# Loading the first group's x of a spectral filter and spatial-shift MLP kernel through two issuing engines

## The chip, the cores and the metric

The kernel runs on one core of a Trainium2 chip. The core has a matrix engine (PE, with its weight loads shown as PEld), a vector engine (DVE), an activation engine (ACT), a general engine (POOL) and a sync engine (SP) that issues the loads and stores; 16 DMA engines move the data. The metric is the device time of one execution in microseconds (us). Before the change it is 407.98, the median of three runs from 407.47 to 408.54.

## What is computed

The input x has 2048 rows of 448 channels. It is normalised over the channels, and the normalised rows go through two branches, whose results are added to x:

```python
x = A_x
xn = _layernorm(x, axis=-1)
return x + _A_ref(xn, A_w_r, A_w_i) + _B_ref(xn, B_w1, B_w2, B_w3, B_w4)
```

The first branch is a spectral filter: a two-dimensional real Fourier transform, a product with complex weights, and the inverse transform. The second is an MLP whose first steps are what the opening of the kernel works on; the part left out shifts each quarter of the channels of h by +1, -1, +2 or -2 rows, as g0 to g3:

```python
def _B_ref(x, w1, w2, w3, w4):
    h = _gelu(_layernorm(x, axis=-1) @ w1)
    ...
    hs = jnp.concatenate([g0, g1, g2, g3], axis=-1) @ w2
    x1 = x + hs
    h2 = _gelu(_layernorm(x1, axis=-1) @ w3) @ w4
    return x1 + h2
```

## The kernel before

**Tiling.** The 2048 rows are viewed as 128 partitions of 16 consecutive rows each; "block b" is row b of each partition, a tile of 128 x 448. Four groups of four blocks are formed (line 22): group 0 is blocks 14, 15, 0 and 1, and groups 1 to 3 follow with blocks 2 to 13. Each group has its own tile `xt[g]` of 128 x 4 x 448 in fp32. For group 0 the blocks lie in two places of x, so `load_x(0)` (lines 195 to 200) issues two loads of two blocks each; the other groups take one load each.

**The opening.** In the order of the source: a one-column tile `warm` is cleared by DVE and run through the gelu on ACT (lines 183 to 185), which makes ACT load its table at the start; DVE clears `wsrc`, the source of PE's warm-up products (line 188), and `ones`; POOL helps to build `ident`. Then SP issues the loads: x of group 0 (two), three pieces of w1 (line 206), its last 64 rows (207), x of group 1, the last 64 rows again into the other 64 partitions (209), w2 (210), x of group 2, and w3 in pieces with x of group 3 between them (221 to 223). PE runs 18 warm-up products of 128 x 512 (lines 900 to 906).

**The chain to the first product.** ACT squares the four pieces of w1 and sums them (lines 951 to 953); PE adds up the sums (`norm_of`, line 965), and DVE makes a power-of-two scale from the result (`factors`, lines 263 to 274). Meanwhile `norm1(0, ...)` (lines 341 to 408) takes each block's mean and variance on DVE (lines 326 and 327), a first guess of the reciprocal root (305) and the negative mean times it (362), and normalises the four blocks in place, three on DVE and one on POOL (370). PE transposes them (428), ACT and DVE split the transposed blocks into two fp16 parts (438, 439), the scaled w1 is split in the same way (281 and 283), and PE starts the products with w1 (479). These go on into w2, w3 and w4, with the Fourier transforms between them, to the end of the kernel.

**The order.** A planner sets the order on each engine. It simulates the program's times (`schedule_with_timeline_sim=True`, line 1220) and takes instructions by their place in the source as they become ready; `with behind(...)` blocks force an instruction behind another one on its engine. The planner also assigns semaphores: in the trace, eight of them serve the loads in turn.

Of the kernel before, what the change touches and what calls it, by code (L numbers as in the profile page):

```python
# [12 lines left out]
F32 = mybir.dt.float32  # L13
F16 = mybir.dt.float16
I32 = mybir.dt.int32
AF = mybir.ActivationFunctionType
# [5 lines left out]
GRP = [[14, 15, 0, 1], [2, 3, 4, 5], [6, 7, 8, 9], [10, 11, 12, 13]]  # L22
# [100 lines left out]
def body(tc, nc, x, wf, w1, w2, w3, w4, c_g, c_n, c_small, out):  # L123
    V, A, P, T, SY = nc.vector, nc.scalar, nc.gpsimd, nc.tensor, nc.sync
# [13 lines left out]
    def pool(name, bufs=1, side="left", space=None):  # L138
        kw = dict(name=name, bufs=bufs, reuse_waits="tile")
        if space is not None:  # L140
            kw["space"] = space
        else:
            kw["side"] = side
        cm = tc.tile_pool(**kw)
        opened[name] = cm
        return cm.__enter__()
# [9 lines left out]
    pc = pool("pc")  # L156
# [6 lines left out]
    xt = [px.tile([128, 4, D], F32, name=f"xt{i}") for i in range(4)]  # L163
# [5 lines left out]
    xv = x.rearrange("(a b) d -> a b d", b=NB)  # L169
    ov = out.rearrange("(a b) d -> a b d", b=NB)  # L170

    def stage(name, n, side, dtype=F32):
        t = pw.tile([128, 1808], F32, tag=f"stage{side}", bufs=1, name=name)
        return (t if dtype is F32 else t.bitcast(dtype))[:, :n]
# [5 lines left out]
        used[0] += 1  # L180
        return xr[:, 452 * (used[0] % 2):452 * (used[0] % 2) + 452]

    warm = pc.tile([128, 1], F32, name="warm")
    V.memset(warm, 0.0)
    A.activation(out=warm, in_=warm, func=AF.Gelu_apprx_tanh)
    x2mem = pw.tile([128, 9 * F], F16, name="x2mem")
    wsrc = x2mem[:, 8 * F:8 * F + 512]
    V.memset(wsrc, 0.0)
# [6 lines left out]
    def load_x(g):  # L195
        if g:
            SY.dma_start(xt[g], xv[:, GRP[g][0]:GRP[g][0] + 4])
        else:
            for i in (0, 2):
                SY.dma_start(xt[g][:, i:i + 2], xv[:, GRP[g][i]:GRP[g][i] + 2])  # L200

    load_x(0)
    w1s = stage("w1s", F, 0).rearrange("p (t n) -> p t n", t=4)
    w2s = stage("w2s", F, 1).rearrange("p (t n) -> p t n", t=4)
    for t in range(3):
        SY.dma_start(w1s[:, t], w1[128 * t:128 * t + 128])
    SY.dma_start(w1s[0:64, 3], w1[384:448])
    load_x(1)
    SY.dma_start(w1s[64:128, 3], w1[384:448])
    SY.dma_start(w2s[:112], w2)  # L210
    load_x(2)
    w3raw = pa.tile([128, 4, F], F32, tag="R", bufs=1, name="w3raw")

# [823 lines left out]
    for k in (1, 3):  # L1037
        with behind(0, 3):
            A.activation(out=w2p[:, 0, k], in_=w2s[:112, k], func=AF.Copy)
        with behind("np", 2):  # L1040
            i = P.tensor_tensor(out=w2p[:, 1, k], in0=w2s[:112, k], in1=w2p[:, 0, k], op=ALU.subtract)
# [182 lines left out]
```

## Time and profile before

| | |
|---|---|
| median of 3 runs | 407.98 us |
| lowest and highest | 407.47 and 408.54 us |
| profiled execution, its own time | 407.72 us |
| its span (first to last instruction) | 405.9 us |
| PE busy | 400.4 us (99%) |
| DVE, ACT, POOL busy | 304.2, 267.5, 170.1 us |
| granted TensorE clock | 1.0 |
| moved by DMA | 49.46 MB |

The profile records one execution. The span leaves out 1.8 us of that execution's own time, which lie around it. "Busy" counts the time in which an engine runs instructions that compute; issuing a load is not counted. The chain of waits is followed back from the last instruction: at each step to what released it, or to the instruction before it on its engine. In the rows of the timeline the columns are start, length, engine, line of the source, operation, written tile <- read tiles, count, and in brackets the idle time of the engine before the row with what ended it. Matmuls are pipelined, and a record of one is longer than its distance from the next.

### The profile page before, as it was taken

The page shows a single profiled execution, that of the slowest core. Times are in us where ns is not written, and L with a number is a line of the kernel's source. Part 1 is how long each engine was busy: PE and PEld are TensorE (multiplying, and loading weights), DVE is VectorE, ACT ScalarE, POOL GpSimd, SP SyncE. Part 2 cuts the span into 40 slices and gives each one's busy share as a digit, 9 for nine tenths or more (in the row PEclk, how much of TensorE's full clock was granted, in tenths as well). Part 3 has the DMA queues.
Part 4 walks back from the last instruction along what each step waited for, and adds up shares of the span by engine and source line. Part 5 has one row for each costly group of instructions (what it writes and reads, how often), then busy time and mean ns, then how long its engine had stood idle before and what let it go on. Part 6 is the DMA issues. An engine that isn't in the chain of part 4 may idle for free.

```text
span 405.9 us, 8826 instructions
## 1 busy us (share of the span) xinstructions
PE 400.4 (99%) x3383; PEld 296.7 (73%) x3383; DVE 304.2 (75%) x657; ACT 267.5 (66%) x464; POOL 170.1 (42%) x269
## 2 busy tenths in 40 slices
PE   8999999999999999999999999999999999999996
PEld 4555556666677877776878878877788888888885
DVE  5989999899645658884677777773588879889645
ACT  4699985874738766862687888776856566444332
POOL 2889911011397746599143344331232164221000
PEclk9999999999999999999999999999999999999999
DMA  8999999906910383427064566631000112233201
GB/s 282 364 267 186 172 178 246 274 2 131 232 48 1 97 277 129 115 39 173 15 157 120 144 158 158 155 94 57 2 1 2 31 61 76 94 108 94 89 2 45
DMA packets 57209, 49.46 MB, mean 122 GB/s; under 512 B 41312, under 2 KB 52192, under 8 KB 57168
## 3 DMA queue, kind: packets, MB, share of 16 engines
q1 hardware_dynamic: 57168, 48.91, 46.1%
q8 instruction: 26, 0.43, 0.4%
q14 instruction: 15, 0.12, 0.1%
HBM read 35.06 MB, written 3.67 MB: 95 GB/s over the span
## 4 chain that ended last, share of the span: by engine, by line
PE 86%; DVE 8%; DMA 3%; ACT 1%; issue 1%; SPq 0%; DVEq 0%
PE pw L449 28%; PE acc L826 22%; PE pw L524 9%; PE pw L479 8%; PE pu L722 3%; PE ps L619 3%; PE pp L676 2%; PE px L693 2%; PE cr L841 2%; PE acc L841 2%; DVE xr L574 1%; DMA out<-xr 1%; PE pe L742 1%; PE py L764 1%; DVE hf L792 1%
## 5 line engine op out<-in xcount | busy, mean ns | idle before, releaser
L449 PE MATMUL pw<-x2mem,w3p 128*128 128x256 f16 x1232 | 149.1, 272 | 0.0
L449 PEld LDWEIGHTS <-w3p 128*128 128x128 f16 x1232 | 118.7, 98 | 19.3
L826 PE MATMUL acc<-w4p,hf 128*128 128x448 f16 x508 | 107.4, 352 | 0.0
L826 PEld LDWEIGHTS <-hf 128*128 128x128 f16 x532 | 51.4, 98 | 35.6
L792 DVE SCALAR_TENSOR_TENSOR hf<-pw,h,hf 128x512 f16<-128x512 f32 x56 | 41.8, 747 | 36.2 <-ACT hf L791 35.8
L788 ACT ACTIVATE pw<-pw,pe 128x512 f32<-128x512 f32 x56 | 36.7, 655 | 44.0 <-PE pw L449 43.8
L791 ACT ACTIVATE hf<-pw,h 128x512 f16<-128x512 f32 x56 | 38.2, 683 | 1.2
L524 PE MATMUL pw<-w2p,h 112*128 112x448 f16 x192 | 38.9, 352 | 0.0
L749 POOL TENSOR_TENSOR e<-e 128x226 f32<-128x226 f32 x16 | 10.7, 669 | 64.3 <-ACT e L746 56.9
L479 PE MATMUL pw<-w1p,w4x 128*128 128x448 f16 x176 | 34.8, 352 | 0.5 <-DVE pe L270 0.5
L524 PEld LDWEIGHTS <-h 112*128 112x128 f16 x192 | 18.8, 98 | 15.6
L703 POOL TENSOR_TENSOR xr<-te 128x450 f32<-128x450 f32 x16 | 15.7, 980 | 34.1 <-DVE te L701 34.1
L479 PEld LDWEIGHTS <-w4x 128*128 128x128 f16 x176 | 17.1, 98 | 16.4 <-ACT w4x L438 0.7
L711 POOL TENSOR_TENSOR zb<-xr,zb 128x450 f16<-128x450 f32 x16 | 16.1, 1009 | 17.1 <-ACT zb L710 17.1
L756 ACT ACTIVATE vh<-e 128x448 f16<-128x448 f32 x16 | 9.2, 576 | 15.7 <-DVE e L754 15.6
L699 DVE SCALAR_TENSOR_TENSOR te<-px,sc,wc 128x450 f32<-128x450 f32 x16 | 11.0, 685 | 10.3 <-ACT te L698 6.7
L698 ACT ACTIVATE te<-px 64x450 f32<-64x450 f32 x32 | 17.2, 539 | 1.7 <-PE px L693 1.2
L734 ACT ACTIVATE U<-y 113x512 f16<-113x512 f16 x32 | 18.0, 620 | 0.1
L746 ACT ACTIVATE e<-pe 128x452 f32<-128x452 f32 x16 | 8.7, 544 | 13.0 <-PE pe L742 10.2
L726 DVE SCALAR_TENSOR_TENSOR y<-pu,y 113x512 f16<-113x512 f32 x16 | 10.9, 687 | 6.9 <-ACT y L725 6.8
L757 DVE TENSOR_TENSOR vh<-e,vh 128x448 f16<-128x448 f32 x16 | 10.0, 622 | 7.1 <-ACT vh L756 7.1
L683 ACT ACTIVATE pf<-pp 64x450 f16<-64x450 f32 x16 | 8.7, 541 | 9.7 <-PE pp L676 7.8
(205 smaller groups left out, 784.3 us busy)
## 6 DMA issues: line engine op xcount, KB each, us to landing
wc<-wf SPq DMA_DIRECT2D x32, 225.0 KB, 3.8
wl<-wf SPq DMA_DIRECT2D x8, 450.0 KB, 4.1
xt<-x SPq DMA_DIRECT2D x3, 896.0 KB, 10.8
w3raw<-w SPq DMA_DIRECT2D x3, 896.0 KB, 13.9
xf<-x SPq DMA_DIRECT2D x6, 448.0 KB, 3.8
xr<-x SPq DMA_DIRECT2D x12, 224.0 KB, 2.5
out<-xr SPq DMA_DIRECT2D x12, 224.0 KB, 2.0
gn<-c_g SPq DMA_DIRECT2D x16, 128.0 KB, 3.3
```

Of the source, the lines that this page charges most:

```text
L449: m = T.matmul(ps_out, wp[:, wi + t, cols], xT[:, xi + t, tok], start=t == 0 and wi + xi == 0, stop=t == 3 and wi == 4)
L479: m = T.matmul(pm[:, :D], xTs[g][:, xi + t, 128 * i:128 * i + 128], w1p[:, wi + t], start=t == 0 and p == 0, stop=t == 3 and p == 2)
L524: m = T.matmul(w2b[b][:, :D], hT[g][:112, 4 * hi + k, o:o + 128], w2p[:, wi, k], start=k == 2 and hi + wi == 0, stop=k == 3 and hi == 1)
L698: i = A.activation(out=e[64 * h:64 * h + 64], in_=px_[64 - 64 * h:128 - 64 * h, :2 * DF], func=AF.Copy)
L703: P.tensor_tensor(out=z, in0=t[:, 0], in1=t[:, 1], op=ALU.add)
L711: P.tensor_tensor(out=zv[1], in0=z, in1=zv[0], op=ALU.subtract)
L734: A.activation(out=U[b][:113, p].rearrange("p q (c k) -> p q c k", c=NC), in_=Y1[:113, p, :, :, b], func=AF.Copy)
L788: A.activation(out=pm, in_=pm, func=AF.Gelu_apprx_tanh, scale=r3)
L791: i = A.activation(out=h[:, 0], in_=pv_, func=AF.Copy, scale=h3)
L792: j = V.scalar_tensor_tensor(out=h[:, 1], in0=pv_, scalar=h3, in1=h[:, 0], op0=ALU.mult, op1=ALU.subtract)
L826: m = T.matmul(to, h[:, hi, 2 * f + i], w4p[0][:, wi, 2 * fp + f, r], start=fp == s and f == 0 and hi + wi == 0, stop=fp == e and f == 1 a ...
L841: m = T.matmul(to, h[:, hi, slot] if slot < 4 else g[:, hi, slot - 4], w4f[fp][k][wi], start=k in (0, 6) and fp == 0 and hi == 0, stop=hi ...
```

## The change

The second of the two loads of group 0 is issued by ACT (`A`) in place of SP (`SY`). The clearing of `warm` and its activation, which brings ACT's table load with it, move from ahead of the memsets to behind `load_x(0)`, so that ACT's issue stands ahead of them in the source. Nothing else is changed; the loads move the same bytes to the same places.

```diff
-    warm = pc.tile([128, 1], F32, name="warm")
-    V.memset(warm, 0.0)
-    A.activation(out=warm, in_=warm, func=AF.Gelu_apprx_tanh)
     x2mem = pw.tile([128, 9 * F], F16, name="x2mem")
     wsrc = x2mem[:, 8 * F:8 * F + 512]
     V.memset(wsrc, 0.0)
...
         if g:
             SY.dma_start(xt[g], xv[:, GRP[g][0]:GRP[g][0] + 4])
         else:
-            for i in (0, 2):
-                SY.dma_start(xt[g][:, i:i + 2], xv[:, GRP[g][i]:GRP[g][i] + 2])
+            for i, q in ((0, SY), (2, A)):
+                q.dma_start(xt[g][:, i:i + 2], xv[:, GRP[g][i]:GRP[g][i] + 2])

     load_x(0)
+    warm = pc.tile([128, 1], F32, name="warm")
+    V.memset(warm, 0.0)
+    A.activation(out=warm, in_=warm, func=AF.Gelu_apprx_tanh)
```

## The prediction

> **What bounds the kernel now.** I read the page first, for the engine that fills the span and for what lies outside it.
>
> ```profile
> span 405.9 us, 8826 instructions
> PE 400.4 (99%) x3383; PEld 296.7 (73%) x3383; DVE 304.2 (75%) x657; ACT 267.5 (66%) x464; POOL 170.1 (42%) x269
> ```
>
> PE is busy for 99% of the span, so time can be won or lost in three places only: before PE gets going, in holes between its matmuls, and after its last one. A split of the span into stretches (length, then busy time and count of each engine, granted clock, DMA share, GB/s) shows where the holes are.
>
> ```profile
> 2.00:3.00 1.00, 1.00 (x4) 0.40 (x3) 0.00 (x0) 0.21 (x2) 0.59 (x2) 1.00 0.64 179
> 3.00:4.00 1.00, 1.00 (x4) 0.36 (x3) 0.00 (x0) 0.00 (x0) 0.00 (x0) 1.00 0.93 362
> 6.00:13.00 7.00, 6.21 (x43) 4.36 (x42) 6.76 (x23) 5.05 (x13) 3.42 (x5) 1.00 1.05 327
> 13.00:20.00 7.00, 7.00 (x41) 3.94 (x40) 6.67 (x22) 3.93 (x6) 6.40 (x17) 1.00 1.00 397
> 20.00:30.00 10.00, 10.00 (x61) 5.67 (x59) 8.60 (x24) 9.23 (x18) 8.17 (x17) 1.00 1.10 271
> 40.00:405.90 365.90, 362.43 (x3180) 275.76 (x3178) 270.80 (x552) 237.85 (x413) 140.69 (x185) 1.00 0.41 105
> 402.70:405.90 3.20, 0.00 (x0) 0.00 (x0) 0.45 (x1) 0.00 (x0) 0.00 (x0) 1.00 0.41 143
> ```
>
> Between 13 and 30 us PE has no hole. From 40 us on it lacks 365.90 - 362.43 = 3.47 us, of which 3.20 is the stretch after its last matmul. About 0.3 us is left in all that time: whatever moves PE's first real matmul moves the end by the same amount. So the chain of waits over the first 11 us decides (start, length, what).
>
> ```profile
> 0.73 3.93 DMA xt<-x
> 4.66 0.02 issue
> 4.68 1.15 DVE sta L326 x2
> 5.84 0.22 DVE mva L327 x2
> 6.05 1.04 DVE sta L326 x2
> ...
> 7.95 1.87 DVE xt L370 x4
> ...
> 10.38 0.45 DVE w1p L281
> 10.84 0.07 DVE pe L270
> 10.91 0.07 issue
> 10.98 0.92 PE pw L479 x4
> ```
>
> The first link is the landing of the first half of group 0 (blocks 14 and 15) at 4.66. From there DVE works through 6.30 us without a break: statistics, normalisation, scale of w1, and PE's first product with w1 at 10.98. The second half (blocks 0 and 1) isn't a link: DVE goes from the first half's averages at 5.84 to the second half's statistics at 6.05 with no wait named. Asked for singly, the two issues (size, us from issue to landing) read
>
> ```profile
> xt<-x SPq DMA_DIRECT2D x1, 448.0 KB, 3.9
> xt<-x SPq DMA_DIRECT2D x1, 448.0 KB, 4.6
> ```
>
> and the first instructions in order of time (start, length)
>
> ```profile
> 0.73 1.28 ACT L185 ACT_TABLE_LOAD   x1 [0.73 <-PEq L1217]
> 0.80 0.06 DVE L184 MEMSET warm<- 128x1 f32 x1 [0.80 <-PEq L1217]
> 0.89 0.27 DVE L188 MEMSET x2mem<- 128x256 uint32 x1
> 1.19 0.42 SPq L200 DMA_DIRECT2D xt<-x  x1
> 1.66 0.42 SPq L206 DMA_DIRECT2D w1s<-w  x1
> 2.02 0.20 ACT L185 ACTIVATE warm<-warm 128x1 f32<-128x1 f32 x1
> 5.76 0.35 SPq L197 DMA_DIRECT2D xt<-x  x1
> 6.42 0.58 ACT L246 ACTIVATE xr<-w1s 128x448 f16<-128x448 f32 x1 [4.20 <-DMA w1s<-w]
> ```
>
> The second half, issued at 1.19, lands 4.6 later, near 5.74: 1.08 us after the first. 448 KB in 1.08 us is about 425 GB/s, close to what the stretches after 3 us show. The two halves come one behind the other at the pace of the DMA engines, and only the front one holds up DVE.
>
> **The change, part by part.**
>
> *One issue leaves SP.* The second half's row at 1.19 disappears there, and everything behind it comes 1.66 - 1.19 = 0.47 us sooner: the w1 pieces, x of group 1, w2, x of group 2, w3. This gains nothing: from 3 us on the DMA share is 0.93 to 1.10, so an earlier place in a full queue is no earlier landing. The squares of w1 on ACT wait for those pieces, and their norm meets DVE's chain here:
>
> ```profile
> 9.68 0.28 PE L967 MATMUL pm<-m,ones 128*128 128x1 f32 x2
> 10.01 0.15 DVE L265 TENSOR_SCALAR pe<-pm 128x1 int32<-128x1 int32 x1
> ```
>
> The norm's last product ends at 9.96 and DVE reads it at 10.01, so the two paths are level: an earlier w1 alone can't pull PE forward, nor does a w1 that comes no later hold up a DVE that starts later.
>
> *One issue enters ACT.* ACT issues for about 0.42 us (the row at 1.19), then loads its table for 1.28, then runs the one-column activation for 0.20: it is free at about 0.73 + 0.42 + 1.28 + 0.20 = 2.63 instead of 2.22. What hides this is its idle time of 4.20 us up to 6.42; without that cover it would cost 0.42. Behind the issue on ACT stands nothing but these two and the squares.
>
> *The memset of the one-column tile moves behind the others on DVE.* The 512-column source of PE's warm-up is cleared up to 0.09 us sooner (0.89 - 0.80), and PE's warm-up begins and ends as much sooner. It is worth nothing, since PE waits for the norm afterwards.
>
> *Loads that wait for earlier landings.* SP's tenth load (group 2's x) starts at 5.76, right after the second load landed at 5.74. If the ninth hangs on the first half in that way and that lands at 5.6, it goes out some 0.8 later than now. At that time nearly 1.5 MB (w1 and group 1's x) is still queued, over 3 us at 400 GB/s: no cost as long as that queue is there.
>
> *Two transfers in flight at once.* This is the part with a price, and no row shows two queues at work side by side. If the second half's packets go out at the same time as the first half's, the first no longer has the engines to itself. Lower bound: its packets still go first, and it lands at 4.66, for 0. Upper bound: the two are mixed evenly and end together, with all the bytes of both moved, which is when the second half lands now, 5.74: +1.08. Below nothing: a second queue could fill the thin start. In the slice from 2 to 3 us the engines move 179 GB/s, against 362 in the next, so (362 - 179) / 362 = 0.5 us of transfer is missing there. If all of it were filled, both halves would be in at 5.74 - 0.5 = 5.24, still 0.6 behind 4.66; only a start filled on top of an undisturbed first half would gain, and I allow 0.3 for it. I take +0.9, near the upper end: both issues start within some hundredths of a us, since SP and ACT both start at 0.73, so neither half has a lead, and I grant the second queue a third of the thin start.
>
> The Trainium skill ("DMA: Bandwidth & Descriptors", section "Queues, rings and completion order") says that SP and ACT each own one ring on each of the same 16 DMA engines, and that an engine goes round its rings packet by packet; its section "Issuing engines are not separate DMA queues" says that issuing from several engines only saves the sequencer's time. By that rule the saved 0.47 us of issue buys no bandwidth, the halves mix, and the sum would be between +0.9 and +1.08; the 425 GB/s between the landings agrees with a shared limit, but no run here yet has two rings.
>
> *What the delay carries along.* All of DVE's 6.30 us starts 0.9 later, at about 5.6, with the second half there as well, so its statistics follow without a new wait. PE's first product goes from 10.98 to about 11.9. ACT's squares then have 0.9 to spare. Since PE has no hole between 13 and 30 us and 0.3 us after 40, nothing takes the delay up.
>
> The sum against the profiled execution: its span of 405.9 becomes 406.8, and its own time of 407.72, which has 1.8 us around the span, 408.6. That execution is 0.26 under the median of the runs, 407.98; the forecast on the median is 408.9, or +0.22%.
>
> **The rivals.**
>
> *The clock of PE falls back.* Place: the stretch from the end of the warm-up to the first product. These rows (duration of a record, least/median/most, of the warm-up before and after 5.2 us; then the stretches of PE alone) tell its price.
>
> ```profile
> L904 PE MATMUL wps<-x2mem x10: 478/634/634, 1.2 to 5.0; 128*128 128x512 f16 x10
> L904 PE MATMUL wps<-x2mem x10: 379/379/634, 4.6 to 6.9; 128*128 128x512 f16 x10
> 1.20:5.30 4.10, 4.08 (x10) 1.00 0.82 269
> 5.30:7.30 2.00, 2.00 (x12) 1.00 1.13 370
> 7.30:8.30 1.00, 0.73 (x7) 1.00 0.88 292
> 8.30:11.00 2.70, 2.18 (x17) 1.00 1.07 358
> ```
>
> Ten warm-up matmuls take the first 4.1 us, and then the same matmul goes about twice as fast, though the granted clock reads 1.00 throughout. PE is now thinly used from 7.3 to 10.98, with 0.27 + 0.52 us of holes; the change stretches this by 0.9, into holes of up to 1 us. Decisive is whether PE's work falls under what keeps it fast. If so, another 4.1 us at half pace lose about 2.05: 407.98 + 0.9 + 2.1 = 411.0. For it: only small products are in this stretch. Against it: the squares' products and the norm's two warming matmuls stay in between. The Trainium skill ("TensorE: Matmul & The Clock Gate", section "Part 1: The HAM clock gate") has the clock halve after an idle window of some 3.4 us; by that rule no hole here is long enough, and this case would not come about.
>
> *The first half keeps its lead.* If each engine finishes the first half's share before it turns to the other queue, or ACT's queue starts late, DVE starts at 4.68 as before: 408.0. For it: SP's issue at 0.73 isn't touched. Against it: ACT starts at 0.73 as well, so the lead would have to arise in all 16 engines; one that takes the second half first holds the landing up.
>
> *The second queue fills the thin start.* The first half lands up to 0.3 sooner: 407.7. Against it: more bytes compete for the same start.
>
> *The change doesn't do what it says.* The table load stays ahead of the issue; the second half goes out at 2.0 instead of 1.19 and lands at about 6.2 to 6.5, and DVE, ready for it at 6.05, waits 0.2 to 0.4: 408.3.
>
> *Another order of the instructions.* The order on each engine is planned from modelled times, and these change for a dozen loads. The least that a worse order costs is one DVE piece ahead of PE's first product (0.45 to 1.04 in the chain), on top of the delay: 409.9. A better one could win the holes of 0.27 + 0.52 us before 10.98 and the 0.3 later, 1.1 at most: 406.9, if the delay isn't there.
>
> **How the numbers follow.** Chances: the forecast 0.48; the clock 0.12; lead kept 0.12; thin start filled 0.07; table first 0.04; another order 0.17, of which 0.07 better and 0.10 worse. What a measurement of this kernel can tell from no change is about 0.3%, 1.2 us. The forecast's own range is 408.4 to 409.6 (+0.4 to +1.1 of delay, and half a us for the runs, which lie 1.07 us apart); I put 0.30 of its 0.48 within 1.2 us of before and 0.18 over it. Slower by over 0.3%: 0.18 + 0.12 + 0.10 and 0.01 of table first, 0.41. Faster: 0.07 + 0.02 of the thin start, 0.09. Within: 0.50. The range from 407.2 to 410.6 leaves out most of the clock's case and the better order, about 0.17.
>
> **What would show it.** In the changed kernel the chain of waits should start with x's landing near 5.6, not 4.66, the two halves' landings should lie within 0.2 us of each other, DVE's statistics should begin right there, and PE's first product with w1 should stand near 11.9, with the order of DVE's instructions unchanged. ACT should show its table load near 1.2, and its first square no later than 6.42 by more than a few tenths. If the first half still lands at 4.7, the step on sharing is wrong. If PE starts near 11.9 and the end doesn't move by as much, the claim that nothing takes it up is wrong. Warm-up records of 634 ns behind 7 us, or products with w1 at twice their spacing, would speak for the clock; a different sequence on DVE or PE, for the order.

## The result and the profile after

| | before | after |
|---|---|---|
| median of 20 runs each | 407.93 us | 408.70 us |
| lowest and highest | 407.10 and 408.71 | 408.06 and 410.15 |
| profiled execution, its own time | 407.72 | 408.60 |
| its span | 405.9 | 406.8 |
| first half of group 0 in | 4.66 | 5.92 |
| PE's first product with w1 | 10.98 | 12.25 |

The ratio of after to before is 1.0024, with a 95% interval from 1.0016 to 1.0033: about 1.0 us slower, 0.65 to 1.35. The medians differ by 0.77 only, because the slowest six executions of the changed kernel weigh more in the ratio. The sequence of instructions is the same on PE and POOL in both kernels; on DVE, ACT and SP it differs only in what the change itself moves. So the time went by way of waits.

The chain of waits of the changed kernel (start, length, what) begins with a longer landing:

```profile
0.74 5.19 DMA xt<-x
5.92 0.02 issue
5.95 1.15 DVE sta L326 x2
7.10 0.22 DVE mva L327 x2
7.32 1.04 DVE sta L326 x2
...
9.21 1.87 DVE xt L370 x4
...
11.65 0.45 DVE w1p L281
12.11 0.07 DVE pe L270
12.18 0.07 issue
12.25 0.92 PE pw L479 x4
```

Every link behind the landing has the length that it had before: 12.25 - 5.95 = 6.30 us, as 10.98 - 4.68. The whole loss is in the first row, 5.92 - 4.66 = 1.26 us. The issues, singly (size, us to landing), and the traffic from 3 to 4 us by queue (q1 is SP's, q10 ACT's) say why:

```profile
xt<-x ACTq DMA_DIRECT2D x1, 448.0 KB, 5.0
xt<-x SPq DMA_DIRECT2D x1, 448.0 KB, 5.2
q1 hardware_dynamic: 55, 0.20, 48.3%
q10 hardware_dynamic: 53, 0.19, 46.9%
```

Both go out at 0.73 to 0.74, and while they are under way the engines serve the two queues in equal parts, 55 packets to 53. The halves come in together, near 5.75 and 5.92, each about as late as the second one alone was before (5.74).

ACT's own instructions, in order of time, cost nothing, as forecast:

```profile
0.73 0.40 ACTq L197 DMA_DIRECT2D xt<-x  x1
1.16 1.28 ACT L202 ACT_TABLE_LOAD   x1 [1.16 <-PEq L1217]
2.45 0.20 ACT L202 ACTIVATE warm<-warm 128x1 f32<-128x1 f32 x1
6.39 0.58 ACT L246 ACTIVATE xr<-w1s 128x448 f16<-128x448 f32 x1 [3.74 <-DMA w1s<-w]
```

In the split by stretches (length, busy time and count of each engine, clock, DMA share, GB/s) the thin start is a little fuller than before, 222 against 179 GB/s and 387 against 362, and the end is as tight:

```profile
2.00:3.00 1.00, 1.00 (x4) 0.43 (x3) 0.00 (x0) 0.65 (x2) 0.60 (x2) 1.00 0.77 222
3.00:4.00 1.00, 1.00 (x4) 0.32 (x3) 0.00 (x0) 0.00 (x0) 0.00 (x0) 1.00 0.95 387
13.00:20.00 7.00, 7.00 (x42) 4.06 (x41) 6.80 (x20) 4.45 (x7) 6.58 (x15) 1.00 1.00 391
40.00:406.80 366.80, 363.52 (x3187) 276.53 (x3185) 271.91 (x556) 239.45 (x413) 142.79 (x191) 1.00 0.41 105
403.55:406.80 3.25, 0.00 (x0) 0.00 (x0) 0.45 (x1) 0.00 (x0) 0.00 (x0) 1.00 0.40 141
```

The first product is 1.27 later, the span only 0.9 longer. From 40 us on, PE now lacks 366.80 - 363.52 = 3.28 us, 3.25 of them after its last matmul: the 0.27 of holes that stood in the profile of before are down to 0.03. That is 0.24 of the missing 0.4. Whether a late start closes that hole, or this execution merely lacked it, is a question for the experiments.

The list of all 20 executions of the changed kernel raises a second one. In 14 the mean granted clock is 0.998 to 1.000, and their median is 408.62. In the other 6 it is 0.994 to 0.996, and they take 409.25 to 410.15, with a median of 409.82.

### The profile page after: what moved, and what is told of

Read it like the earlier page. It is cut to its first block, busy times and chain, and to the rows that moved or that the text cites. A ratio compares the mean times of both kernels' runs of the same rounds, so it can differ in the third digit from the quotient of the medians.

```text
span 406.8 us, 8826 instructions
## 1 busy us (share of the span) xinstructions
PE 400.7 (98%) x3383; PEld 297.0 (73%) x3383; DVE 304.0 (75%) x657; ACT 267.7 (66%) x464; POOL 171.0 (42%) x269
## 4 chain that ended last, share of the span: by engine, by line
PE 96%; DVE 2%; DMA 1%; issue 0%
PE pw L449 33%; PE acc L826 24%; PE pw L524 9%; PE pw L479 8%; PE cr L841 4%; PE acc L841 3%; PE pu L722 3%; PE ps L619 3%; PE pp L676 2%; PE pe L742 2%; PE px L693 2%; PE py L764 2%; DMA xt<-x 1%; PE pta L428 1%; PE end L826 1%; DVE sta L326 1%
## 5 line engine op out<-in xcount | busy, mean ns | idle before, releaser
L749 POOL TENSOR_TENSOR e<-e 128x226 f32<-128x226 f32 x16 | 11.3, 708 | 63.9 <-ACT e L746 60.6
L598 POOL TENSOR_TENSOR xr<-xf 128x452 f32<-128x452 f32 x6 | 6.7, 1124 | 19.7 <-issue 10.1
```

## The experiments

Three theories stood at the start: that the two halves share the DMA engines and the first pays for it; that part of a late start is taken up near 376 us; and that the granted clock falls in some executions because PE is thinly used for longer. Each ratio is to runs of the kernel before on the same chip. "First product" is that of each kernel's profiled execution.

### Which part of the change costs the time

**The move of the memset and the activation alone**, on the changed kernel:

```diff
-            for i, q in ((0, SY), (2, A)):
-                q.dma_start(xt[g][:, i:i + 2], xv[:, GRP[g][i]:GRP[g][i] + 2])
+            for i in (0, 2):
+                SY.dma_start(xt[g][:, i:i + 2], xv[:, GRP[g][i]:GRP[g][i] + 2])
```

> The one-column tile and its activation stand behind the loads, both halves stay on SP. Theory (the delay is the two halves sharing the DMA engines): as before, first half in at 4.6 to 4.8, first product with w1 at 10.9 to 11.1, ratio to before 0.999 to 1.001. Rival (the moved memset, activation and table load cost time): first product 0.3 or more later, ratio 1.001 to 1.002.

Measured: first half in at 4.4, first product at 10.73, both some 0.2 earlier than expected; ratio 0.9996 (0.9986 to 1.0005). The move costs nothing that these runs can tell; the queue does.

**ACT's issue behind its table load**, on the kernel before:

```diff
-    A.activation(out=warm, in_=warm, func=AF.Gelu_apprx_tanh)
+    warmed = A.activation(out=warm, in_=warm, func=AF.Gelu_apprx_tanh)
...
-            for i in (0, 2):
-                SY.dma_start(xt[g][:, i:i + 2], xv[:, GRP[g][i]:GRP[g][i] + 2])
+            SY.dma_start(xt[g][:, 0:2], xv[:, GRP[g][0]:GRP[g][0] + 2])
+            with tc.issue_after(warmed.ins):
+                A.dma_start(xt[g][:, 2:4], xv[:, GRP[g][2]:GRP[g][2] + 2])
```

> ACT issues the second half, but only behind its table load and activation, at about 2.2 instead of 0.73. Theory (sharing): the first half's packets run alone at the start, so it lands at 4.7 to 5.2 instead of 5.92; the second half comes at 5.8 to 6.5 and DVE may wait for it; first product at 11.0 to 11.7, ratio 1.000 to 1.002. Rival (SP's w1 pieces, 0.47 us sooner behind the first half, cause the delay): first half at 5.7 to 6.0 as in the changed kernel, first product at 12.1 or later.

Measured: ratio 1.0004 (0.9994 to 1.0013). Its chain, and the traffic of its two queues from 3 to 4 us:

```profile
0.73 4.07 DMA xt<-x
4.81 0.02 issue
4.83 1.15 DVE sta L327 x2
...
11.22 0.92 PE pw L480 x4
```

```profile
q1 hardware_dynamic: 79, 0.25, 71.6%
q10 hardware_dynamic: 28, 0.10, 30.1%
```

From 2 to 3 us ACT's queue moves nothing at all (42 packets, all on q1). With that lead the first half is in at 4.81, though the second half uses ACT's queue and SP's w1 pieces come as early as in the changed kernel. So neither ACT's queue as such nor the earlier w1 makes the delay; being in flight at the same time does. The rival falls.

**The two halves exchanged**, on the changed kernel:

```diff
-            for i, q in ((0, SY), (2, A)):
+            for i, q in ((0, A), (2, SY)):
```

> ACT issues the first half, SP the second with everything else behind it. Theory (sharing): it doesn't matter which queue carries which half, both land at 5.6 to 6.0, first product at 11.9 to 12.4, ratio 1.0015 to 1.003. Rival (the first half is late because w1 stands behind it on its own queue): alone on ACT's queue it lands at 5.2 or sooner, first product 11.6 or sooner.

Measured: ratio 1.0016 (1.0005 to 1.0027), 2 of 12 executions at a granted clock of 0.995, 54 packets on q10 and 52 on q1 from 3 to 4 us, and the chain

```profile
0.73 4.90 DMA xt<-x
5.63 0.02 issue
5.66 2.20 DVE sta L326 x4
...
11.82 0.92 PE pw L479 x4
```

The first half has ACT's queue to itself and is late all the same: sharing again. The first product is 0.1 earlier than expected.

**The changed kernel again, unaltered.**

> The changed kernel again, unaltered, for a second execution's landing beside the kernel before on one chip. Theory (mixing): the two halves land at 5.4 to 6.0 and within 0.3 of each other, first product at 11.7 to 12.4, 2 to 5 of 12 executions at 0.994 to 0.996, ratio 1.0016 to 1.0035. Rival (the 5.92 of the first profile was a chance): a landing under 5.2.

Measured: halves in near 5.5 and 5.7, first product at 12.01, ratio 1.0030 (1.0018 to 1.0041), 3 of 9 executions at 0.994 to 0.996. The late landing wasn't a chance of one profile.

**Half as much on ACT's queue**, on the changed kernel:

```diff
-            for i, q in ((0, SY), (2, A)):
-                q.dma_start(xt[g][:, i:i + 2], xv[:, GRP[g][i]:GRP[g][i] + 2])
+            SY.dma_start(xt[g][:, 0:2], xv[:, GRP[g][0]:GRP[g][0] + 2])
+            for i, q in ((2, A), (3, SY)):
+                q.dma_start(xt[g][:, i:i + 1], xv[:, GRP[g][i]:GRP[g][i] + 1])
```

> Only block 0 (224 KB) goes over ACT's queue at the start; blocks 14 and 15 in one load and block 1 behind it stay on SP. Theory (two queues at work at once share the engines packet by packet, so the first half pays for the bytes on ACT's queue): half the delay of the changed kernel, landing at 5.1 to 5.4 instead of 5.92 and 4.66, first product at 11.4 to 11.8. Rival (a second queue at the start costs a fixed time, whatever it carries): landing at 5.7 or later.

Measured: first half in at 5.61, between the two expectations; first product at 11.87; ratio 1.0034 (1.0021 to 1.0046), with 3 of 6 executions at 0.995 to 0.996. From 3 to 4 us the queues read (packets, MB, share)

```profile
q1 hardware_dynamic: 70, 0.25, 68.3%
q10 hardware_dynamic: 69, 0.12, 31.6%
```

The turns are equal in packets, not in bytes: ACT's packets are half as large here, and its 224 KB are as many packets as the 448 KB of the first half. So the smaller load doesn't leave the first half's way as early as its bytes suggest. That alone doesn't give 5.61, and how the delay grows with the bytes on the second queue stays open.

### What becomes of a late start

Here no load is touched. One, two or three needless statistics instructions stand on DVE ahead of the first real one, in the kernel before (n is 1, 2, 3):

```diff
-    n1 = [norm1(0, [V, V, P, V])]
+    dst = pc.tile([128, 6], F32, name="dst")
+    for k in range(n):
+        i = V.bn_stats(out=dst, in_=xb(GRP[0][0]))
+    with tc.issue_after(i.ins):
+        n1 = [norm1(0, [V, V, P, V])]
```

> The kernel before, with one more statistics instruction (0.58 us) on DVE ahead of the first, no load touched. Theory (a part of any delay of the first product is taken up later, in a hole of PE near 376 us which another chain sets): first product at 11.4 to 11.7, ratio 1.000 to 1.0008 (0 to 0.35 us). Rival (nothing takes it up): ratio 1.0012 to 1.0017 (0.5 to 0.7 us).

> The same with two more statistics instructions (1.15 us), about the delay of the changed kernel without its loads. Theory (the loads matter only through DVE's late start): first product at 12.0 to 12.3, ratio 1.0015 to 1.0030 as in the changed kernel, and 1 to 5 of 12 executions at a granted clock of 0.994 to 0.996 with 409.3 us or more. Rival (the lower clock comes from ACT's queue or the table load): none of them under 0.998.

> The kernel before with three more statistics instructions (1.7 us) on DVE, no load touched. Theory (a later start of DVE's chain reaches the end in full and by its length alone lets the clock fall): first product at 12.2 to 12.7, ratio 1.004 to 1.006, at least 2 in 12 executions at 0.994 to 0.996. Rival (a later stretch takes a part up): ratio 1.002 to 1.0035. Rival for the clock (it needs ACT's queue): none under 0.998.

| more on DVE (its own length) | first product | ratio (interval) | executions under 0.998 |
|---|---|---|---|
| 0.58 | 10.91 | 1.0011 (1.0003 to 1.0020) | 0 of 12 |
| 1.15 | 11.81 | 1.0045 (1.0032 to 1.0058) | 1 of 5 |
| 1.73 | 12.53 | 1.0074 (1.0050 to 1.0098) | 4 of 6 |

In the first two the first product came earlier than expected, since x landed at 4.2 and 4.4 in their profiles. From DVE's start to the first product these profiles need 6.69, 7.35 and 8.01 us, against 6.30 in the kernel before, so what the additions really delay is 0.39, 1.05 and 1.71. The first run alone is inconclusive: +0.45 us lies between the two expectations, which took the delay for 0.58, and is no less than the 0.39. The other two speak against my theory that something takes the delay up. Among the executions at full clock, 1.15 more on DVE costs 1.2 us (409.0 against a median of 407.78, four executions), and 1.73 costs 1.65 (409.73 against 408.08, two executions). Both ratios came out above the range expected, in part because the clock falls in some of the rest. The hole near 376 us is still there in both profiles (PE waits 0.3 us for DVE's hf, as before), and in the changed kernel's second profile too, so a late start by itself doesn't close it.

The profiles of all these kernels say the same. In the eleven taken at full clock the span less the first product lies between 394.6 and 395.8 us. It averages 395.2 for the four whose first product comes by 11.3, and 395.0 for the seven with a later one, so at most a few tenths of a late start are taken up.

### Where the clock falls

**Fewer warm-up products**, on the kernel before, so that nothing is late but PE's thin stretch begins sooner:

```diff
-WARM = 18
+WARM = 13
```

> The kernel before with 13 instead of 18 warm-up products: PE's thin stretch begins 1 us sooner and its end stays. Theory (the length of the thin stretch lets the clock fall): first product at 10.7 to 11.1 as before, but at least 2 in 12 executions at 0.994 to 0.996 and 409 us or more, ratio 1.0005 to 1.002. Rival (only a later first product does it): as before, none under 0.998, ratio 0.999 to 1.001.

Measured: 6 of 11 executions at 0.994 to 0.996, with a median of 408.74, against 407.66 for the other five; ratio 1.0002 (0.9992 to 1.0012). The ratio is under what was expected, and none of the six reaches the expected 409 us; but the rival falls: no queue and no late load is needed. The profiled execution is one of the six, and the stretches of PE alone show the place (its first product, at 11.43, is late for this reason):

```profile
5.70:9.10 3.40, 2.42 (x16) 1.00 1.06 377
9.10:12.50 3.40, 3.31 (x13) 0.50 1.06 289
12.50:20.00 7.50, 7.50 (x44) 1.00 1.00 367
```

For 3.4 us the granted clock is half. The same in the one-block kernel's profile, with the stretch of the changed kernel's first profile, where the clock stayed, in the second fence:

```profile
7.30:10.70 3.40, 2.28 (x16) 1.00 0.98 309
10.70:14.10 3.40, 3.33 (x15) 0.50 1.04 246
14.10:20.00 5.90, 5.90 (x35) 1.00 1.00 389
```

```profile
10.70:14.10 3.40, 2.88 (x23) 1.00 1.00 259
```

15 matmuls instead of 23 get done from 10.7 to 14.1. The Trainium skill ("TensorE: Matmul & The Clock Gate", section "Part 1: The HAM clock gate") calls the window 3.4 us long and free-running, not tied to the kernel's start; by that, an execution would fall or not by chance of phase, that is, by where in its windows it starts. The length agrees with the 3.4 us here, and the fall comes in a part of the executions. The phase shows too: the records of the warm-up products shorten from 634 to 380 ns at about 5.7 us in the first of these profiles and from 631 to 379 at about 3.9 in the one-block kernel's, and the clock falls 3.4 and 6.8 us later, one and two windows. The condition that the Trainium skill gives there for the half clock, an idle window, does not agree: PE had records in 2.42 and 2.28 of the 3.40 us ahead of the falls. Thin use was enough.

How thin it must be, the time covered by records doesn't tell. In the profile of the exchanged halves the warm-up gets fast at about 5.0, and its second window, with much the same share of records, kept the clock:

```profile
8.43:11.85 3.42, 2.39 (x17) 1.00 1.06 317
11.85:15.26 3.41, 3.41 (x22) 1.00 0.99 301
```

A record is longer than the matmul's turn on PE. A rough estimate takes for each matmul its distance from the next where they run back to back in these traces: 0.22 us for a warm-up product, 0.19 for a product with w1, 0.11 for a transpose, 0.03 for a product of one column. By it PE was in use for 1.2 to 1.5 of the 3.4 us ahead of the three falls that were profiled (these two, and one in the kernel of four loads below), and for 1.5 to 2.8 in the first two windows of the other profiles. A limit near 1.5 would fit both, but no run here tests it.

**More warm-up** and **warming later**, both on the changed kernel:

```diff
-WARM = 18
+WARM = 24
```

> The changed kernel with 24 instead of 18 warm-up products, about 1.3 us more of warm-up in PE's hole. Theory (besides the later landing, the granted clock falls to 0.994 to 0.996 in 6 of 20 executions of the changed kernel, which then take about 1.2 us longer): no execution under 0.999, first product still at 12.1 to 12.4, the slowest execution under 409.3, ratio 1.0015 to 1.002. Rival (the executions over 409 us have another cause): as many at a lower clock as before, slowest at 410.

```diff
-    warm_on(n1[0][3], 2)
+    warm_on(n1[0][3], 6)
```

> The changed kernel with 6 instead of 2 warming products behind the norm, in the hole of PE from 9.9 to 10.5. Theory (the clock falls where PE is thinly used between 7.3 and 12.3, and these keep it up): at most one execution in 12 at 0.994 to 0.996, first product at 12.1 to 12.4, ratio 1.0013 to 1.002. Rival (four more products aren't enough, or the cause lies elsewhere): 3 or more of 12 at 0.994 to 0.996, ratio 1.002 to 1.003.

Measured: 24 products give 3 of 12 executions at 0.994 to 0.996 and a ratio of 1.0023 (1.0011 to 1.0036); the expectation failed. They end too early to keep PE in use until the first product, and PE itself becomes a link of the chain: its first half was in at 5.46, yet the first product stands at 12.27.

```profile
1.19 8.09 PE wps L904 x24
9.28 0.56 PE pm L967 x6
...
12.27 0.92 PE pw L479 x4
```

Six products behind the norm gave no fall in 5 executions, which are few (at the changed kernel's 9 in 29, five without a fall come by chance about once in six times). The ratio is 1.0039 (1.0027 to 1.0051), above both expectations: the norm's products queue behind them, and the first product comes at 12.53. As a remedy neither pays.

### A try at something faster

**Group 0 in four loads**, all on SP, in the kernel before:

```diff
-            for i in (0, 2):
-                SY.dma_start(xt[g][:, i:i + 2], xv[:, GRP[g][i]:GRP[g][i] + 2])
+            for i in range(4):
+                SY.dma_start(xt[g][:, i:i + 1], xv[:, GRP[g][i]:GRP[g][i] + 1])
```

> The kernel before with group 0 in four loads of one block each, all on SP in order. Theory (what lands first decides, and one queue serves its loads in order): the first block lands 0.3 to 0.5 sooner than the first half of before (4.2 to 4.66 in the runs so far), but PE's first product moves forward by 0.1 at most, since the norm of w1 is level with DVE's chain: ratio 0.998 to 1.001. Rival (four issues push w1 back by 0.9 and its norm becomes the bound): first product 0.3 or more later, ratio 1.001 to 1.0025.

Measured: ratio 1.0060 (1.0044 to 1.0075), 3 of 6 executions at 0.996. The first block is in at 3.3, a full 1.4 before the first half of before, and it is worth nothing: PE waits 2.0 us for ACT's squares of w1, which come late, and the first product stands at 12.71. The rival had the right mechanism and too small a price. Part of the price is a slump of the DMA engines in this profile,

```profile
3.00:3.50 0.50, 0.50 (x3) 0.20 (x2) 0.21 (x1) 0.00 (x0) 0.00 (x0) 1.00 1.09 355
3.50:5.25 1.75, 1.75 (x6) 0.56 (x4) 1.05 (x3) 0.00 (x0) 0.00 (x0) 1.00 0.94 198
```

busy for 0.94 of the time at half the rate. Its cause is not known. No version here beats the kernel before.

## Why the prediction was right, and where it wasn't

The forecast was 408.9 us, +0.22%, with a range from 407.2 to 410.6; measured were 408.70 and +0.24%. By its steps:

- **What bounds the kernel.** "Whatever moves PE's first real matmul moves the end by the same amount" held: two and three instructions added on DVE, which put off the first product by 1.05 and 1.71, cost 1.2 and 1.65 at full clock. In the first pair of profiles 0.24 us did vanish in the hole that I had counted as 0.3 and then left out; but a delay doesn't close it as a rule.
- **The issue off SP and the memset's place: nothing.** Shown by the first experiment (0.9996) and by the second, where w1 goes out as early as in the changed kernel and the time is that of before.
- **The issue on ACT: hidden.** ACT is free at 2.65, as worked out (2.63), and its first square starts at 6.39 instead of 6.42.
- **Later loads that hang on earlier landings.** The ninth load went out at 5.76, just behind ACT's landing, some 1.0 later than before, and no load starved.
- **Two transfers in flight at once.** The mechanism is shown: 55 packets to 53, both halves in together, the same with the halves exchanged, and gone when one has a lead. The size was off. I took +0.9 of a bound of +1.08 and granted the second queue a third of the thin start. The two profiles of the changed kernel have the first product 1.27 and 1.03 later. Over more profiles the term is larger still: in five with two whole halves on two queues the first half lands at 5.4 to 6.0, in five with one queue at 4.2 to 4.7, on the average about 1.3 apart. The thin start did fill by about what I granted, (222 - 179) + (387 - 362) = 68 KB or 0.17 us, but the bound was no bound: it took the landing of the second half before, 5.74, for the moment at which both must be in, and 5.92 is later. In that profile only 2 packets of ACT's queue are left from 5.0 to 5.5 us, beside 120 on SP's, which by then carries w1: so the end of the delay looks like the tail of a few late packets rather than the shared rate.
- **Why the sum came out.** At full clock the changed kernel's median is 408.62, +0.69 on 407.93; in 9 of 29 executions in two sets of runs the fall of the clock adds some 1.2 (409.82 against 408.62), 0.4 on the average. 0.7 and 0.4 make 1.1, and the interval is 0.65 to 1.35. That the number came so close is thus in part luck: the forecast put all of its +0.9 on the first product, which moved by more and cost less at full clock, and nothing on the clock. That the first product comes over 1.0 later in both profiles and the end of the full-clock executions only 0.7 later is not settled; two profiles are few, since the landing in kernels with one queue alone lies between 4.2 and 4.7.
- **The clock rival.** I gave it 0.12, as an outcome of its own for the whole kernel. It is not that: it comes in a part of the executions, and it cost 1.2, not 2.1. In what I listed as its condition, the longer thin stretch, it was right: fewer warm-up products alone bring it about, while among executions of before on these chips 1 of 73 shows it.
- **Lead kept, thin start gained, another order.** The first is real, but needs ACT to be late: it is the second experiment. The other two did not come about.

## What to carry to other kernels

Before a load is moved to a second queue, ask who waits for the load that stays: two queues that started together shared the engines here packet by packet, and the piece that the chain needed first then landed when both did. Here one queue in the order of need gave it the lead for nothing, and the issue time saved on a queue that was already full was worth nothing. And where PE is kept warm ahead of its first real work, a delay of one microsecond cost a second one through the clock here, in a part of the executions; so look at the list of executions, not at the median alone.

## What the runs showed of the hardware beyond that

- A load issued by ACT behind an activation is recorded early and moves late. In the second experiment its row stands at 0.91, while the activation ahead of it ends at 2.23; its queue has no packet from 2 to 3 us and 28 from 3 to 4. The record of an issue on ACT is not the start of the transfer.

```profile
0.91 0.37 ACTq L201 DMA_DIRECT2D xt<-x  x1
2.03 0.20 ACT L185 ACTIVATE warm<-warm 128x1 f32<-128x1 f32 x1
```

- The granted clock fell to 0.50 for 3.4 us in three of the profiles though PE had no hole over 1 us in the 3.4 us ahead, and in the kernel with 1.73 us more on DVE two executions lost about twice as much (mean clock 0.991).
